# Delta-rule attention with a quick-GELU feed-forward on one core: scores, substitution and key normalization moved to other places of a slot

## The chip, the core and the metric

The kernel runs on one core of one Trainium2 chip. The metric is device time in microseconds (us) of one execution, the median of several runs. The core has a matrix engine (PE, with its weight loads shown apart as PEld), three engines for elementwise work (DVE, ACT, POOL) and DMA queues, which SP and ACT issue here. Each engine works off its own instructions in the order in which the program holds them, and waits on semaphores for the others.

## The reference

Two blocks, one behind the other. The first is delta-rule attention over 4 batches, 8 heads, 768 tokens and a head size of 48, with the keys normalized first:

```python
k_n = k / (np.linalg.norm(k, axis=-1, keepdims=True) + 1e-06)
state = np.zeros((B, H, D, D))
for t in range(S):
    kt, vt, bt = (k_n[:, :, t], v[:, :, t], beta[:, :, t, None])
    y[:, :, t] = np.einsum('bhd,bhde->bhe', q[:, :, t], state)
    v_old = np.einsum('bhde,bhd->bhe', state, kt)
    state = state + bt[:, :, :, None] * np.einsum('bhd,bhe->bhde', kt, vt - v_old)
```

The second takes the result as 3072 rows of 384 numbers:

```python
h = x @ w_in                                  # 384 x 2048
g = h * (1.0 / (1.0 + np.exp(-1.702 * h)))
return g @ w_out                              # 2048 x 384
```

q, k, v and beta are float32. w_in and w_out are float64, and the kernel turns them into float32 on its own engines.

## The kernel before

**Units and chunks.** The 768 tokens are cut into 6 chunks of 128, and a unit is one chunk of one batch with all 8 heads: 24 units, chunk by chunk, batch by batch. Inside a chunk the recursion becomes a triangular system, solved in 4 blocks of 32 rows.

**What a unit needs, in order.** Its keys (`KN`, 7 buffers) and queries (`QP`, 3 buffers) are loaded. `normalize` scales the keys: POOL squares them (`ksq`), DVE sums the squares (`ssq`), POOL takes the root with a power (`rn`), DVE adds 1e-6 and inverts, POOL multiplies. `prepare` is the scores of a unit. It transposes keys and queries on PE (`psT`), ACT copies them (`kqT`), PE forms key-key and key-query products in two halves (`psG`), ACT and DVE copy them (`G`), and two DMAs carry the key-key blocks through DRAM (`Nd`) into the layout `NT`. It is a generator that stops four times, after each transpose and after each half of the products. `invert` is the substitution, the inverse of the diagonal blocks. It is all DVE: one product with beta, 15 steps of product and sum, 8 larger products and sums, and a last product `YS` that goes out and back by DMA as `XB`. It is a generator of 25 stops, and one call serves two units.

**The sequence proper** is the class `Step`: `above` (products of earlier blocks, `psR`), `rest` (DVE subtracts, `V<-V,psR`), `solve` (PE, `psU`), `solved` (ACT copies to `U`), `queries`, `state` (`psS`, and DVE adds into `S_bd`) and `outputs` (`psY`, copied to `last` and `xT`).

**Slots.** `slot(n, share)` has six groups (places). It works on three units at once: the last two blocks and the state of unit n-1 (A), the second block of unit n (B_) and the first block of unit n+1 (D_). Beside them it puts the scores of unit n+4, steps of the substitution, the conversion of weights (early slots) and, from a queue, matmuls of the feed-forward (`hidden`, `ph`; `written`, `po`), 20.8 units of cost a slot in the long run. Before the change the scores stand in the first, second, fourth and fifth place; a substitution starts in the first place of each even slot with 4 stops a place, and what is left runs at the slot's end. Also at the end the next keys are loaded and normalized in one go.

**Order.** A scheduler merges this program order into one order for each engine. Calls wrapped in `pinned` keep their place in program order. So what an engine does in which order is read from the built kernel, not from the code alone.

**Start.** Four units are prepared first, then one substitution over all four (128 partitions) runs on DVE, while PE has only filler (`warm`). Keys of units 4 to 6 are loaded after that work's DMAs on SP; units 4 and 5 are normalized in a pinned block on DVE, unit 6 with `normalize`.

Of the kernel before, what the change touches and what calls it, by code (L numbers as in the profile page):

```python
# [18 lines left out]
def kernel(  # L19
# [19 lines left out]
    nc = tc.nc  # L39

    B, H, S, D = q.shape
# [10 lines left out]
    HB = 2  # L52
    GR = 6
# [22 lines left out]
    units = [(c, b) for c in range(NC) for b in range(B)]  # L76


    KN = [cpool.tile([128, H, DP], F32, name=f"KN{i}") for i in range(7)]
    QP = [cpool.tile([128, H, DP], F32, name=f"QP{i}") for i in range(3)]  # L80
# [5 lines left out]
    def load(n, pairs, dma=nc.sync.dma_start):  # L86
        c, b = units[n]
        for dst, src in pairs:
            dma(
                out=dst[n % len(dst)][:, :, 0:D],  # L90
                in_=src[b, :, c * C : (c + 1) * C, :].rearrange("h p d -> p h d"),
            )
# [9 lines left out]
    def pinned(op):  # L102

        return lambda *a, **kw: tc.keep_in_program_order(op(*a, **kw))  # L104
# [146 lines left out]
    ready = {}  # L251
    inverse = {}

    def normalize(n, mul):
        K = KN[n % len(KN)][:, :, 0:D]
        ksq = wk.tile([128, H, D], F32, tag="ksq", name="ksq", bufs=1)
        mul(ksq, K, K, op=ALU.mult)
        ssq = wk.tile([128, H], F32, tag="ssq", name="ssq", bufs=4)
        nc.vector.tensor_reduce(ssq, ksq, axis=AX.X, op=ALU.add)  # L259
        rn = wk.tile([128, H], F32, tag="rn", name="rn", bufs=4)  # L260
        nc.gpsimd.tensor_tensor(rn, ssq, half, op=ALU.pow)  # L261
        nc.vector.tensor_scalar(rn, rn, 1e-6, None, op0=ALU.add)
        nc.vector.reciprocal(rn, rn)
        mul(K, K, rn.broadcast_to([128, H, D]), op=ALU.mult)

    def normalize_first(b0):

# [7 lines left out]
        for b in range(HB):  # L275
            K = KN[(b0 + b) % len(KN)][:, :, 0:D]
            tt(sq[:, b], K, K, op=mult)
            red(s[:, b], sq[:, b], axis=AX.X, op=add)
# [9 lines left out]
        for b in range(HB):  # L288
            K = KN[(b0 + b) % len(KN)][:, :, 0:D]
            tt(K, K, s[:, b].broadcast_to([128, H, D]), op=mult)  # L290

# [138 lines left out]
    def bank(name, shape=(128, H, D)):  # L430
        return ps_seq.tile(list(shape), F32, tag="seq", name=name)
# [158 lines left out]
    def run(work):  # L590
        for _ in work:
            pass

    def ahead_of(work, n):
        for _ in range(n):
            next(work, None)

    steps, xTs, inverting, gT0 = {}, {}, iter(()), []

    def slot(n, share):  # L600

        nonlocal inverting
        A, B_, D_ = steps.pop(n - 1, None), steps.get(n), None
        P = prepare(n + B) if B <= n + B < len(units) else iter(())
        m = n - HB
        if m >= 0 and m % HB == 0 and m + B < len(units):  # L610
            inverting = invert(*units[m + B], HB)
        left = WB[n + 1] if n + 1 < len(WB) else 0
        todo = share
        for group in range(GR):
            if group == 0:
                if A:
                    for h in range(H):
                        A.above(2, h)
                    A.rest(2)
                next(P, None)  # L620
            elif group == 1:
                psU = bank("psU") if A else None
                for h in range(H):
                    if A:
                        A.solve(2, h, psU)
                    if B_:
                        B_.above(1, h)
                if A:
                    A.solved(2, psU)
                if B_:  # L630
                    B_.rest(1)
                next(P, None)
            elif group == 2:
                if A:
                    for h in range(H):
                        A.above(3, h)
                    A.rest(3)
                if n + 1 < len(units):
                    h = (n + 1) // HB
                    if h not in xTs:  # L640
                        xTs[h] = wk.tile([128, KC, NTH], F32, tag="xT", name="xT", bufs=3)
                    D_ = steps[n + 1] = Step(n + 1, xTs[h])
                    D_.keys()
                    D_.rest(0)
            elif group == 3:
                psU = bank("psU")
                turns = [(X, blk) for X, blk in ((A, 3), (B_, 1), (D_, 0)) if X]
                for h in range(H):
                    for X, blk in turns:
                        X.solve(blk, h, psU)  # L650
                for X, blk in turns:
                    X.solved(blk, psU)
                if A:
                    A.queries()
                next(P, None)
            elif group == 4:
                if A:
                    A.state()
                next(P, None)
                run(P)  # L660
            elif A:
                A.outputs()
            ahead_of(inverting, 4)
            more = left // (GR - group)
            run(weights(more))
            left -= more
            if queue:
                for cost in take(todo / (GR - group)):
                    todo -= cost
            if not queue and n <= HB:  # L670
                warm(NB0)
        if n + 1 == len(WB) - 1:
            run(weights(n_parts))
        run(inverting)
        if n > 0:
            if n - 1 + B < len(units):
                load_values(n - 1 + B)
            m = n - 1 + len(KN)
            if m < len(units):
                load(m, ((KN, k), (QP, q)), sync if n < B else nc.sync.dma_start)  # L680
                normalize(m, nc.gpsimd.tensor_tensor)
            h = (n - 1) // HB
            if h == 0:
                i = (n - 1) % HB
                queue.append(hidden(xTs[h], gT0, slice(i * C, (i + 1) * C), 0.67))
            if n % HB == 0:
                gT = gT0 if h == 0 else []
                if h > 0:
                    queue.append(hidden(xTs[h], gT, slice(0, NTH), 1.3))
                queue.append(written(*units[h * HB], gT))  # L690
                xTs.pop(h)

    queue = []
    sync = pinned(nc.sync.dma_start)
# [17 lines left out]
    nc.gpsimd.memset(S_bd, 0.0)  # L712
    for i in range(B, len(KN)):
        nc.gpsimd.memset(KN[i][:, :, D:DP], 0.0)
    for i in range(B, B + HB):
        load(i, ((KN, k), (QP, q)), sync)
    run(invert(0))
    normalize_first(B)
    for i in range(B + HB, len(KN)):
        load(i, ((KN, k), (QP, q)), sync)  # L720
        normalize(i, nc.gpsimd.tensor_tensor)
    run(weights(W1))
    for n in range(-1, len(units) + 1):

# [32 lines left out]
```

## Time and profile before

| what | value |
| --- | --- |
| median of 3 runs | 907.6 us (902.69 to 909.66) |
| the profiled execution | 905.0 us, its span 903.0 us |
| mean granted PE clock | 0.941 |
| PE busy | 829.3 us, 92% of the span |
| DVE busy | 499.7 us, 55% |
| ACT, POOL busy | 201.9 us, 105.0 us |
| DMA | 55.79 MB, mean 62 GB/s |

The profile records one execution. Busy time is the time in which an engine has an instruction under way. An idle stretch is put down to the engine or DMA that ended it, its releaser. The granted clock is the share of full speed that PE was given; in this profile it is 1 or 0.5, with changes between. Matmul ends are modelled, so PE's busy time is an upper bound of its work.

### The profile page before, as it was taken

How to read it: one execution, taken by the hardware profiler on the slowest of the kernel's cores; microseconds unless marked ns; L12 is line 12 of the kernel's file. 1: busy time of each engine (PE TensorE's matmuls, PEld its weight loads, DVE VectorE, ACT ScalarE, POOL GpSimd, SP SyncE). 2: the span in 40 equal slices, each digit the busy share in tenths (PEclk: the TensorE clock that was granted, in tenths of full speed). 3: DMA queues.
4: the chain of work that ended last, by engine and by line, in shares of the span. 5: the costliest groups of instructions: out<-in, count | busy, mean ns of one | idle time of the engine just before them, and what ended most of it. 6: DMA issues, size and time to landing. Idle time of an engine off the chain costs nothing.

```text
span 903.0 us, 15752 instructions
## 1 busy us (share of the span) xinstructions
PE 829.3 (92%) x6564; PEld 614.9 (68%) x6564; DVE 499.7 (55%) x1044; ACT 201.9 (22%) x387; POOL 105.0 (12%) x92
## 2 busy tenths in 40 slices
PE   8308999989999998998998998998999999999998
PEld 6206778657767766866866866866867767768684
DVE  7698749988993294285286286285286293110000
ACT  3102424332221311321311321321321312112020
POOL 2101101203112102102102102102100000000000
PEclk9658859999999998998999999998999999999999
DMA  9968235354213213213213213213202101000000
GB/s 176 212 83 136 85 91 130 96 124 101 37 40 82 50 36 73 49 36 74 49 28 82 49 28 81 50 33 67 49 20 65 41 19 34 4 20 3 12 9 19
DMA packets 164487, 55.79 MB, mean 62 GB/s; under 512 B 130112, under 2 KB 160064, under 8 KB 164416
## 3 DMA queue, kind: packets, MB, share of 16 engines
q1 hardware_dynamic: 158288, 53.57, 27.5%
q10 hardware_dynamic: 6128, 1.21, 1.1%
q8 instruction: 52, 0.85, 0.4%
q14 instruction: 19, 0.16, 0.1%
HBM read 33.13 MB, written 20.45 MB: 59 GB/s over the span
## 4 chain that ended last, share of the span: by engine, by line
PE 65%; DVE 24%; DMA 3%; issue 3%; POOL 3%; ACT 1%; SPq 1%; ACTq 0%; DVEq 0%
PE ph L536 24%; PE po L551 18%; PE psR L457 5%; DVE P L365 4%; PE psG L318 4%; PE psY L482 4%; PE psU L469 4%; PE psR L446 3%; POOL rn L261 2%; DVE NT L366 2%; DVE YB L366 2%; DVE YB L386 2%; PE psT L304 2%; DVE P L382 2%; PE psS L501 1%
## 5 line engine op out<-in xcount | busy, mean ns | idle before, releaser
L536 PE MATMUL ph<-xT,w_in 128*128 128x256 f32 (+1 forms) x1248 | 271.9, 375 | 0.0
L551 PE MATMUL po<-w_out,gT 128*128 128x384 f32 x768 | 268.3, 495 | 3.8 <-DVE w_out L176 3.8
L536 PEld LDWEIGHTS ph<-xT,w_in 128*128 128x128 f32 x1248 | 224.9, 196 | 35.1 <-issue 7.5
L551 PEld LDWEIGHTS po<-w_out,gT 128*128 128x128 f32 x768 | 140.9, 191 | 95.2 <-issue 9.4
L465 DVE TENSOR_TENSOR V<-V,psR 32x384 f32<-32x384 f32 x92 | 50.6, 550 | 132.7 <-PE psR L457 90.6
L541 ACT ACTIVATE gT<-ph 128x512 f32<-128x512 f32 (+1 forms) x104 | 58.6, 564 | 212.9 <-PE ph L536 212.9
L476 ACT COPY U<-psU 32x384 f32<-32x384 f32 x96 | 45.0, 469 | 197.7 <-PE psU L469 127.7
L342 POOL TENSOR_SCALAR_AFFINE_SELECT G<-G 128x1024 f32<-128x1024 f32 x24 | 28.9, 1204 | 414.8 <-issue 167.7
L457 PEld LDWEIGHTS psR<-U,G 32*32 32x32 f32 (+2 forms) x1152 | 58.4, 115 | 20.3 <-issue 19.1
L138 PE MATMUL ps_warm<-ident 128*128 128x256 bf16 x260 | 36.5, 298 | 37.0 <-DVE ps_warm L104 33.1
L318 PE MATMUL psG<-kqT 48*128 48x256 f32 x384 | 66.4, 434 | 4.0 <-ACT kqT L305 2.2
L469 PEld LDWEIGHTS psU<-V,XB 32*32 32x32 f32 x1536 | 39.5, 108 | 44.6 <-DVE V L465 22.0
L457 PE MATMUL psR<-U,G 32*32 32x48 f32 (+2 forms) x1152 | 68.9, 215 | 0.0
L469 PE MATMUL psU<-V,XB 32*32 32x48 f32 x1536 | 47.0, 208 | 20.4 <-DVE V L465 18.4
L326 DVE COPY G<-psG 128x512 f32<-128x512 f32 x44 | 30.3, 689 | 62.8 <-PE psG L318 62.2
L138 PEld LDWEIGHTS <-ident 128*128 128x128 bf16 x260 | 26.8, 106 | 45.4 <-DVE ps_warm L104 34.3
L382 DVE TENSOR_TENSOR P<-NT,YB 64x2 f32<-64x2 f32 (+4 forms) x150 | 49.9, 333 | 4.8
L386 DVE TENSOR_REDUCE YB<-P 64x2 f32<-64x2 f32 (+4 forms) x150 | 48.0, 320 | 4.7 <-DVE P L382 0.2
L318 PEld LDWEIGHTS psG<-kqT 48*128 48x128 f32 x384 | 39.4, 201 | 16.3 <-issue 4.7
L558 DVE COPY o<-po 128x384 f32<-128x384 f32 x24 | 13.3, 553 | 62.7 <-PE po L551 62.5
L322 ACT ACTIVATE G<-psG 128x512 f32<-128x512 f32 x48 | 28.6, 596 | 67.0 <-PE psG L318 65.6
L261 POOL TENSOR_TENSOR rn<-ssq,half 128x8 f32<-128x8 f32 x18 | 35.5, 1970 | 49.1 <-DVE ssq L259 49.1
(78 smaller groups left out, 682.7 us busy)
## 6 DMA issues: line engine op xcount, KB each, us to landing
Nd<-G SPq DMA_DIRECT2D x24, 512.0 KB, 3.5
w_out<-in_moe_w_out_dram SPq DMA_DIRECT2D x14, 384.0 KB, 3.1
KN<-in_k_dram SPq DMA_DIRECT2D x24, 192.0 KB, 2.7
w_out<-in_moe_w_in_dram SPq DMA_DIRECT2D x24, 192.0 KB, 4.4
V<-in_v_dram SPq DMA_DIRECT2D x24, 192.0 KB, 3.1
out_dram<-o SPq DMA_DIRECT2D x24, 192.0 KB, 2.0
QP<-in_q_dram SPq DMA_DIRECT2D x21, 192.0 KB, 3.7
NT<-Nd SPq DMA_DIRECT2D x24, 128.0 KB, 2.5
```

The source lines that it names most:

```text
L138: nc.tensor.matmul(ps, lhsT=ones[:, 0:128], rhs=ones, start=True, stop=True)
L261: nc.gpsimd.tensor_tensor(rn, ssq, half, op=ALU.pow)
L318: nc.tensor.matmul(ps[hh][:, i], lhsT=kqT[pr, g + i, 0, :], rhs=kqT[pr, g + i, :, :], start=True, stop=True,)
L382: tt(P, diag(Nf, i * BS, [[0, i], [1, i]]), diag(Yf, 0, [[BS, i], [1, i]]), op=ALU.mult,)
L386: red(diag(Yf, i, [[BS, i]]), P, axis=AX.X, op=ALU.add, negate=True)
L457: nc.tensor.matmul(self.psR[r, h, :], lhsT=self.G[a, h, 0, r], rhs=self.U[a, h, :], start=(self.c == 0 and h == 0), stop=True, skip_group_ ...
L465: nc.vector.tensor_tensor(self.V[r], self.V[r], self.psR[r], op=ALU.subtract)
L469: nc.tensor.matmul(psU[r, h, :], lhsT=self.XB[r, h, :], rhs=self.V[r, h, :], start=True, stop=True,)
L476: nc.scalar.copy(self.U[r], psU[r])
L536: nc.tensor.matmul(ph[:, u], lhsT=w_in[:, j, f * 128 : (f + 1) * 128], rhs=xT[:, j, t], start=(j == 0), stop=(j == KC - 1),)
L541: nc.scalar.activation(gT[f0 // FQ][:, f0 % FQ : f0 % FQ + 2, t], ph, ACT.Gelu_apprx_sigmoid)
L551: nc.tensor.matmul(po, lhsT=gT[f // FQ][:, f % FQ, i * C : (i + 1) * C], rhs=w_out[:, f, :], start=(f == 0), stop=(f == FC - 1),)
```

## The change

Four things are done together.

1. In `slot`, the scores of unit n+4 are brought forward: both transposes in the first place, the first half of the products in the second, the second half with its DMAs in the third. Nothing of them is left in the fourth and fifth.
2. A substitution begins in the last place of an odd slot with 5 stops, for units n+3 and n+4, and goes on with 4 stops a place in the even slot; what is left runs at the end of even slots only.
3. `normalize` becomes a generator with three stops: squares; sum and power; addition, reciprocal and product. Slot n takes one step of it a place, for unit n+5, whose keys were loaded at the end of slot n-1. Its products are always POOL's.
4. At the start, keys and queries of units 4 to 6 are loaded by ACT's queue ahead of the first substitution, and unit 6 is normalized in slot 1.

```diff
-    def normalize(n, mul):
+    def normalize(n):
         K = KN[n % len(KN)][:, :, 0:D]
+        mul = nc.gpsimd.tensor_tensor
         mul(ksq, K, K, op=ALU.mult)
+        yield 0.0
         nc.vector.tensor_reduce(ssq, ksq, axis=AX.X, op=ALU.add)
         nc.gpsimd.tensor_tensor(rn, ssq, half, op=ALU.pow)
+        yield 0.0
         nc.vector.tensor_scalar(rn, rn, 1e-6, None, op0=ALU.add)
...
+        yield 0.0
...
-        m = n - HB
-        if m >= 0 and m % HB == 0 and m + B < len(units):
-            inverting = invert(*units[m + B], HB)
+        m = n - 2 + len(KN)
+        K = normalize(m) if B + HB <= m < len(units) else iter(())
...
+                next(P, None)
                 next(P, None)
             elif group == 1:
...
                     D_.rest(0)
+                run(P)
             elif group == 3:
...
                     A.queries()
-                next(P, None)
             elif group == 4:
                 if A:
                     A.state()
-                next(P, None)
-                run(P)
             elif A:
                 A.outputs()
-            ahead_of(inverting, 4)
+            next(K, None)
+            if group == GR - 1 and n % HB == 1:
+
+                m = n + 1 + HB
+                if B <= m < len(units):
+                    inverting = invert(*units[m], HB)
+            ahead_of(inverting, 5 if n % HB == 1 else 4)
...
-        run(inverting)
+        if n % HB == 0:
+            run(inverting)
...
-                normalize(m, nc.gpsimd.tensor_tensor)
...
-    for i in range(B, B + HB):
-        load(i, ((KN, k), (QP, q)), sync)
+    for i in range(B, len(KN)):
+        load(i, ((KN, k), (QP, q)), pinned(nc.scalar.dma_start))
     run(invert(0))
     normalize_first(B)
-    for i in range(B + HB, len(KN)):
-        load(i, ((KN, k), (QP, q)), sync)
-        normalize(i, nc.gpsimd.tensor_tensor)
```

Three places of DVE's order show what the scheduler makes of it. Line numbers behind the change are 1 to 5 higher: `V<-V,psR` is L465 before and L469 after, `NT<-NT,bI` L358 and L362. P, YB, NT and YS belong to the substitution; ssq and rn to the normalization.

The first place is where an even slot passes into an odd one, in the long run. Before:

```order
L366 TENSOR_REDUCE YB<-P 64x16x4
L517 COPY last<-psY 48x128
L518 COPY xT<-psY 48x3x128
L366 TENSOR_REDUCE YB<-P 64x16x4
L259 TENSOR_REDUCE ssq<-ksq 128x8
L416 TENSOR_TENSOR YS<-YB,bI 64x1024
L262 TENSOR_SCALAR rn<-rn 128x8
L465 TENSOR_TENSOR V<-V,psR 32x384
L263 RECIPROCAL rn<-rn 128x8
L558 COPY o<-po 128x384
```

and after:

```order
L369 TENSOR_TENSOR P<-NT 64x1024
L370 TENSOR_REDUCE YB<-P 64x16x4
L420 TENSOR_TENSOR YS<-YB,bI 64x1024
L562 COPY o<-po 128x384
L513 TENSOR_TENSOR S_bd<-psS,S_bd 64x4x48 x2
L521 COPY last<-psY 48x128
L522 COPY xT<-psY 48x3x128
L261 TENSOR_REDUCE ssq<-ksq 128x8
L265 TENSOR_SCALAR rn<-rn 128x8
L266 RECIPROCAL rn<-rn 128x8
L469 TENSOR_TENSOR V<-V,psR 32x384
```

The end of the substitution has moved from behind the copies of the even slot's outputs to ahead of its state update; the subtraction V still stands behind one normalization.

The second place is the middle of an odd slot, where the copies of the scores (`G<-psG`) and the start of the next substitution (`NT<-NT,bI`) stand. Before:

```order
L326 COPY G<-psG 128x2x256
L509 TENSOR_TENSOR S_bd<-psS,S_bd 64x4x48 x2
L326 COPY G<-psG 128x2x256
L259 TENSOR_REDUCE ssq<-ksq 128x8
L262 TENSOR_SCALAR rn<-rn 128x8
L263 RECIPROCAL rn<-rn 128x8
L517 COPY last<-psY 48x128
L518 COPY xT<-psY 48x3x128
L465 TENSOR_TENSOR V<-V,psR 32x384
L358 TENSOR_TENSOR NT<-NT,bI 64x1024
```

and after:

```order
L469 TENSOR_TENSOR V<-V,psR 32x384
L330 COPY G<-psG 128x2x256
L469 TENSOR_TENSOR V<-V,psR 32x384 x2
L330 COPY G<-psG 128x2x256
L362 TENSOR_TENSOR NT<-NT,bI 64x1024
L386 TENSOR_TENSOR P<-NT,YB 64x2
L390 TENSOR_REDUCE YB<-P 64x2
L386 TENSOR_TENSOR P<-NT,YB 64x8
L513 TENSOR_TENSOR S_bd<-psS,S_bd 64x4x48 x2
```

The start of the substitution now follows the last copy of the scores directly, and the state update, the output copies and the next V stand behind it.

The third place is the start: the end of the first weight conversions and the begin of the substitution over four units (128 partitions). Before:

```order
L104 TENSOR_SCALAR tmp<-tmp 128x512 x2
L104 SCALAR_TENSOR_TENSOR tmp<-w_out,tmp 128x512
L104 SCALAR_TENSOR_TENSOR w_in<-w_in,tmp 128x512
L104 TENSOR_TENSOR NT<-NT,bI 128x1024
L104 TENSOR_TENSOR P<-NT,YB 128x2
```

and after:

```order
L104 SCALAR_TENSOR_TENSOR w_in<-w_in,tmp 128x512
L261 TENSOR_REDUCE ssq<-ksq 128x8
L265 TENSOR_SCALAR rn<-rn 128x8
L266 RECIPROCAL rn<-rn 128x8
L104 TENSOR_TENSOR NT<-NT,bI 128x1024
L104 TENSOR_TENSOR P<-NT,YB 128x2
```

The normalization of unit 6 has come ahead of the first substitution; before, it stood behind that and behind the pinned block of units 4 and 5.

## The prediction

> **What bounds the kernel now.** I read the engine totals first (PE busy 92% of the span), then busy time by stage, then PE's waits, then the instructions around the longest of them. By stage; the columns are stretch, length, busy us of PE, PEld, DVE, ACT and POOL with instruction counts, granted PE clock, DMA share, GB/s:
>
> ```profile
> 86.00:285.00 199.00, 188.26 (x1638) 140.31 (x1638) 162.23 (x341) 59.86 (x117) 34.15 (x26) 0.90 0.38 90
> 285.00:341.00 56.00, 56.00 (x437) 41.56 (x437) 29.43 (x64) 13.55 (x26) 6.91 (x6) 1.00 0.21 46
> 341.00:690.00 349.00, 334.73 (x2705) 247.85 (x2704) 195.42 (x388) 76.58 (x147) 50.46 (x40) 0.97 0.23 51
> ```
>
> PE is the bound from 285 us on: without a pause at first, and with 349.00 - 334.73 = 14.3 us of idle time and some lost clock between 341 and 690. PE's waits in 285 to 690 have a single entry (waiting, releaser, us, times, longest):
>
> ```profile
> PE psU L469 <- DVE V L465: 14.3, 5, 3.1
> ```
>
> So all of it is one event, five times: a solve waits for a subtraction on DVE. The timeline of the first one (start, us, engine):
>
> ```profile
> 341.96 0.86 PE L457 MATMUL psR<-U,G 64*32 64x48 f32 x16
> 343.25 2.75 PE L551 MATMUL po<-w_out,gT 128*128 128x384 f32 x8
> 344.93 0.55 DVE L259 TENSOR_REDUCE ssq<-ksq 128x8 f32<-128x384 f32 x1
> 345.52 1.22 DVE L416 TENSOR_TENSOR YS<-YB,bI 64x1024 f32<-64x1024 f32 x1
> 345.57 2.67 POOL L261 TENSOR_TENSOR rn<-ssq,half 128x8 f32<-128x8 f32 x1 [4.54 <-DVE ssq L259]
> 348.27 0.17 DVE L262 TENSOR_SCALAR rn<-rn 128x8 f32<-128x8 f32 x1 [1.53 <-POOL rn L261]
> 348.47 0.55 DVE L465 TENSOR_TENSOR V<-V,psR 32x384 f32<-32x384 f32 x1
> 349.08 0.23 PE L469 MATMUL psU<-V,XB 32*32 32x48 f32 x1 [3.08 <-DVE V L465]
> ```
>
> psR was there at 342.8, but V ran at 348.5: in front of it DVE had ssq, the last product YS of the substitution and a wait for POOL's power. PE's cover, the eight po matmuls, ended at 346.0. The price is more than the idle time. From the end of that cover to the end of the 24 ph matmuls behind it, at the five stalls and at the one boundary (689.13) that has no substitution any more:
>
> ```profile
> 346.00:360.57 14.57, 11.49 (x84) 10.01 (x85) 3.33 (x7) 1.66 (x3) 3.07 (x2) 0.77 0.32 64
> 415.85:429.76 13.91, 11.41 (x84) 10.18 (x85) 2.75 (x7) 1.66 (x3) 2.49 (x2) 0.75 0.34 67
> 485.03:497.99 12.96, 9.88 (x84) 8.75 (x85) 3.33 (x7) 1.67 (x3) 3.07 (x2) 0.87 0.35 73
> 553.26:564.04 10.78, 8.27 (x85) 7.44 (x85) 2.76 (x7) 1.67 (x3) 2.50 (x2) 1.00 0.43 86
> 619.32:633.86 14.54, 11.46 (x84) 10.05 (x85) 3.33 (x7) 1.67 (x3) 3.06 (x2) 0.77 0.25 51
> 689.13:697.33 8.20, 8.20 (x84) 7.36 (x85) 1.66 (x3) 1.66 (x3) 0.00 (x0) 1.00 0.44 90
> ```
>
> The same work takes 8.20 us undisturbed; the five sum to 66.76, so the stalls cost 66.76 - 5 x 8.20 = 25.8 us: 14.3 idle, 11.5 from the clock that is halved after four of them.
>
> **The long run, part by part.** *Substitution begun earlier.* DVE's order now has YS ahead of the even slot's state update, so that the V of the odd slot stands behind output copies and one normalization only. For this the scores must be there in time:
>
> ```profile
> 337.62 0.69 DVE L326 COPY G<-psG 128x512 f32<-128x512 f32 x1
> 338.38 0.37 SPq L330 DMA_DIRECT2D Nd<-G  x1
> 341.60 0.34 SPq L336 DMA_DIRECT2D NT<-Nd  x1
> DMA to landing us min/median/max: 2.4/2.5/2.7
> 373.65 0.69 DVE L326 COPY G<-psG 128x512 f32<-128x512 f32 x1 [0.38 <-PE psG L318]
> 381.58 1.22 DVE L358 TENSOR_TENSOR NT<-NT,bI 64x1024 f32<-64x1024 f32 x1
> ```
>
> From the last G copy's end (338.3) to NT's landing are 341.6 + 2.5 - 338.3 = 5.8 us. In the odd slot at 373.65 DVE did not begin until 381.58, 7.2 us behind the copy. Now the copy comes two places earlier, some 10 us of a slot of 32, and NT follows it directly: DVE waits about 5.8 us at its head and then starts roughly 12 us earlier than before. Behind that wait stand S_bd, last and xT, which PE first feeds in the fifth and sixth place; the wait lies mostly beside the solves of the fourth place, where DVE has nothing else. I cost it at nothing; if NT lands later than some 6 us beyond that, it holds the outputs and the next V (rival E). The backlog of 3.1 us at the odd slot's V is gone with 12 us to spare, less the pieces of normalization now ahead of it.
>
> *Keys normalized step by step.* Same instructions, other places. In an even slot the sums of squares stand ahead of last, xT and V, and the keys are loaded only once the state matmuls of the odd slot have freed their buffer.
>
> ```profile
> KN<-in_k_dram SPq DMA_DIRECT2D x24, 192.0 KB, 2.7
> L261 POOL TENSOR_TENSOR rn<-ssq,half 128x8 f32<-128x8 f32 x18 | 35.5, 1970 | 49.1 <-DVE ssq L259 49.1
> 373.58 2.79 PE ph L536 x12
> 338.17 1.08 PE L482 MATMUL psY<-G,U 128*48 128x128 f32 x16
> 342.76 0.66 PE L304 MATMUL psT<-ident,KN 128*128 128x128 f32 x4
> ```
>
> From the end of psS: load 2.7, squares 0.83, ssq 0.55, power 1.97, rn, last and xT 1.0, five substitution pieces about 1.7, V 0.55, and about 1 us of semaphores and issue: 10.3 us. PE has in that stretch, by its new order, three blocks of twelve ph (8.4), four po (half of 2.75), the outputs (1.08), above (0.86) and both transposes (1.3): 13.0 us. The slack is 2 to 3 us, the smallest that I find, and it is what is late next. I leave 2 us of residual stalls over five pairs; the ends are 0 and five stalls like the cheapest above, 5 x (10.78 - 8.20) = 12.9.
>
> POOL's normalization now runs beside the substitution. The last large product of the substitution, beside which POOL squares and selects at the end of an even slot, and an earlier one of the same size without (count, busy us, mean ns):
>
> ```profile
> L365 DVE TENSOR_TENSOR P<-NT 64x1024 f32<-64x1024 f32 x10 | 15.3, 1530 | 0.0
> L365 DVE TENSOR_TENSOR P<-NT,YB 64x1024 f32<-64x1024 f32 x10 | 12.2, 1219 | 0.3
> ```
>
> That is 0.31 us more for a product, within the slack. The Trainium skill, "SBUF — State Buffer", section "SBUF: two separate sides", speaks against the change here: a GpSimd instruction and a VectorE instruction with two SBUF inputs hold a shared port in turn, each for its whole length. By that rule alone POOL's two normalizations of a pair could hold DVE for their whole length instead of for fractions of it, and the residual would rise from 2 us to rival B's 12.9; the rows show the growth, but only a part of such a length.
>
> *Scores forward.* PE, ACT and DVE do the same work in other places: nothing added, and the copies of G have the wait of the fourth place behind them.
>
> **The start.** Here is a cost. Rows of the start before:
>
> ```profile
> 33.23 0.60 ACT L322 ACTIVATE G<-psG 128x512 f32<-128x512 f32 x1 [1.11 <-PE psG L318]
> 42.20 1.22 DVE L104 TENSOR_TENSOR NT<-NT,bI 128x1024 f32<-128x1024 f32 x1
> 75.15 1.05 SPq L104 DMA_DIRECT2D KN<-in_k_dram  x1
> 81.88 0.82 POOL L257 TENSOR_TENSOR ksq<-KN 128x384 f32<-128x384 f32 x1 [46.63 <-DMA KN<-in_k_dram]
> 82.74 0.55 DVE L259 TENSOR_REDUCE ssq<-ksq 128x8 f32<-128x384 f32 x1 [2.10 <-POOL ksq L257]
> 83.37 2.03 POOL L261 TENSOR_TENSOR rn<-ssq,half 128x8 f32<-128x8 f32 x1 [0.66 <-DVE ssq L259]
> 85.64 0.55 DVE L465 TENSOR_TENSOR V<-V,psR 32x384 f32<-32x384 f32 x1
> 86.21 0.20 DVE L263 RECIPROCAL rn<-rn 128x8 f32<-128x8 f32 x1
> 86.24 0.94 PE L469 MATMUL psU<-V,XB 32*32 32x48 f32 x32 [2.55 <-DVE V L465]
> ```
>
> Unit 6's normalization held DVE and V there, and PE 2.55 us. It now stands ahead of the first substitution, on which everything waits. ssq to reciprocal took 86.41 - 82.74 less 0.55 for V = 3.1 us. Its load is the fifth on ACT's queue, free from 33.83. At 75.15, beside other loads, one took 81.88 - 75.15 = 6.7 us; issued at about 35.5, behind four others of some 0.4 each, it lands at 42.2, and the squares end at 43.1, 0.9 us behind DVE's 42.2. So I add 3.1 + 0.9 = 4.0 us (bounds 0, if NT is as late by itself, and 7, if the loads share the queues with the scores' DMAs) and take off the 2.6: +1.4.
>
> **Stage 86 to 285.** DVE is busy 162 of 199 us and its substitutions release PE; PE is idle 199.00 - 188.26 = 10.7 us, and the clock of 0.90 means 0.20 x 199 = 40 us at half. The order is quite another here. Substitutions begin earlier but meet the same weight conversions; units 1 and 2 lose scores that lay between their solves, and DVE waits for NT. Bounds: nothing gained, or all 10.7 and some 9 of the 20 us that half clock can cost. I take half of the idle time, -5, as the work on DVE is unchanged.
>
> **The sum.** -25.8 + 2 + 1.4 - 5 = -27.4. The profiled execution took 905.0 us (span 903.0 and 2.0 around it) and becomes 877.6; it lies 2.6 below the median of 907.6, so the forecast is 880 us.
>
> **Rivals.** A, the forecast: the five stalls go. 0.60.
>
> B, the wait moves: the even slot's V, behind the load, squares and power of that slot's keys, is late in every pair. For: the slack is small. Against: 10.3 us of work under 13.0 of cover. It decides once the keys land some 3 us later than 2.7. Residual 12.9 in place of 2: 891 us. 0.14.
>
> C, the clock stays low: only the idle time goes. For: the drop at 415.85 follows the same 2.5 us of idle time as at 553.26, where there is none. Against: the boundary at 689.13 has the same small matmuls at full clock. Gain 14.3 in place of 25.8: 891.5 us. 0.07. The Trainium skill, "TensorE: Matmul & The Clock Gate", Part 1, leans to C: it wants idleness of about a whole window of 3.4 us before the clock halves, and the windows run free. Stalls of 2.5 to 3.1 us would then not be the cause, yet four of five here are followed by half clock.
>
> D, the start loses 7 - 2.6 = 4.4 and the early stage gains nothing: +3 and +5 on the forecast, 888 us. 0.08.
>
> E, slower: the wait for NT at DVE's head. SP issues Nd and NT behind output DMAs, and every row behind L362 waits with it. Before, 5.2 us a pair were lost (25.8 / 5). To end above 916.7 the new wait must cost 9.1 + 25.8 = 35 us, 7 a pair, which needs NT to land 5.8 + 6 + 7 = 19 us behind the copy; all measured landings are within 2.7 us. 920 us. 0.04.
>
> F, no change: the stalls are merely re-dealt. About 905 us. 0.07.
>
> **Chances.** A change of under 1% (9 us) can hardly be told from none for this kernel. Faster holds A to D but for the tails of B to D: 0.87. Same: F and such tails, 0.08. Slower: 0.05. The range holds A and most of B to D, 0.8 together. Its low end is the forecast less the early stage's other half and the clock, 5 + 9: 866; the high end is B with D, 891 + 8 = 899.
>
> **What would show it.** Right: between 341 and 660 PE idle under 4 us, clock 1.00, no wait of psU for V; L362 some 6 us behind the second G copy; pairs of slots 63.5 us apart (now 69.85 from 346.00 to 415.85, less 6.4). The first substitution begins at 45 to 47 us instead of 42.2, and no wait for rn near 83. Wrong: psU waiting for V in even slots (B), clock 0.5 without idle time (C), long idle time of DVE before L362 with PE idle too (E), PE idle above 10 us between 86 and 285.

## The result and the profile after

| what | before | after |
| --- | --- | --- |
| median | 906.6 us (4 runs, 902.69 to 909.66) | 875.0 us (4 runs, 870.02 to 880.94) |
| ratio, 95% interval | | 0.966 (0.957 to 0.974) |
| profiled execution, its span | 905.0, 903.0 us | 870.0, 868.0 us |
| mean granted PE clock | 0.941 | 0.969 |
| PE, DVE busy | 829.3, 499.7 us | 803.2, 502.0 us |

A second measurement, further down, gave 872.3 us and a ratio of 0.960 (0.956 to 0.964). The forecast was 880 in a range of 866 to 899. The profiled execution of the changed kernel is the fastest of its four, with a mean clock of 0.969; the others lie between 0.953 and 0.965.

The table of stages of the changed kernel, same stretches and columns as in the prediction:

```profile
86.00:285.00 199.00, 183.39 (x1715) 138.03 (x1716) 164.61 (x342) 62.11 (x123) 36.43 (x26) 0.98 0.40 94
285.00:341.00 56.00, 56.00 (x477) 40.65 (x476) 36.90 (x73) 13.81 (x27) 7.90 (x7) 1.00 0.27 59
341.00:690.00 349.00, 349.00 (x2904) 258.79 (x2903) 206.28 (x420) 82.98 (x160) 42.37 (x38) 1.00 0.23 52
```

Between 285 and 690 PE has neither a pause nor a halved clock. In the early stage, 86 to 285, the two parts of the loss went opposite ways: idle time rose from 10.7 to 199.00 - 183.39 = 15.6 us, while the clock rose from 0.90 to 0.98. That is the surprise of this result.

Rows picked from the timeline of the changed kernel where the first stall was, as an even slot passes into an odd one (start, us, engine):

```profile
324.63 0.28 PE L505 MATMUL psS<-U,KN 128*128 128x96 f32 x1
324.94 1.22 DVE L420 TENSOR_TENSOR YS<-YB,bI 64x1024 f32<-64x1024 f32 x1
...
331.52 0.83 POOL L258 TENSOR_TENSOR ksq<-KN 128x384 f32<-128x384 f32 x1 [11.88 <-DMA KN<-in_k_dram]
332.38 0.55 DVE L261 TENSOR_REDUCE ssq<-ksq 128x8 f32<-128x384 f32 x1 [2.33 <-POOL ksq L258]
332.96 2.75 PE L555 MATMUL po<-w_out,gT 128*128 128x384 f32 x8
333.01 1.64 POOL L263 TENSOR_TENSOR rn<-ssq,half 128x8 f32<-128x8 f32 x1 [0.67 <-DVE ssq L261]
335.12 0.55 DVE L469 TENSOR_TENSOR V<-V,psR 32x384 f32<-32x384 f32 x1
335.54 1.46 PE L540 MATMUL ph<-xT,w_in 128*128 128x256 f32 x6
336.93 0.23 PE L473 MATMUL psU<-V,XB 32*32 32x48 f32 x1
```

YS now runs 10 us ahead of V. The wait for POOL's power is still there, and V still stands behind it; but V ends at 335.67 and PE has po and ph until its solve at 336.93. 1.3 us of slack are left here; one pair of slots later they are 2.5.

The waits at DVE's head for NT, from the timeline of DVE:

```profile
282.36 0.69 DVE L330 COPY G<-psG 128x512 f32<-128x512 f32 x1 [0.56 <-PE psG L322]
288.82 1.22 DVE L362 TENSOR_TENSOR NT<-NT,bI 64x1024 f32<-64x1024 f32 x1 [5.77 <-DMA NT<-Nd]
...
352.27 1.22 DVE L362 TENSOR_TENSOR NT<-NT,bI 64x1024 f32<-64x1024 f32 x1 [5.64 <-DMA NT<-Nd]
...
416.01 1.22 DVE L362 TENSOR_TENSOR NT<-NT,bI 64x1024 f32<-64x1024 f32 x1 [5.79 <-DMA NT<-Nd]
```

DVE waits 5.6 to 5.8 us behind the copy, PE does not. Pairs of slots are 63.45 and 63.74 us apart.

And the start of the changed kernel:

```profile
43.33 0.82 POOL L258 TENSOR_TENSOR ksq<-KN 128x384 f32<-128x384 f32 x1 [7.89 <-DMA KN<-in_k_dram]
46.70 0.20 DVE L266 RECIPROCAL rn<-rn 128x8 f32<-128x8 f32 x1
46.88 1.22 DVE L104 TENSOR_TENSOR NT<-NT,bI 128x1024 f32<-128x1024 f32 x1
72.55 1.22 DVE L420 TENSOR_TENSOR YS<-YB,bI 128x1024 f32<-128x1024 f32 x1
87.76 0.55 DVE L469 TENSOR_TENSOR V<-V,psR 32x384 f32<-32x384 f32 x1
```

Unit 6's normalization holds the first substitution until 46.88 (42.20 before); of these 4.7 us, 87.76 - 85.64 = 2.1 are left at the first V.

### The profile page after: what moved, and what is told of

It is laid out like the page before. It is cut to its first block, busy times and chain, and to the rows that moved or that the text cites. A ratio compares the mean times of both kernels' runs of the same rounds, so it can differ in the third digit from the quotient of the medians.

```text
span 868.0 us, 15729 instructions
## 1 busy us (share of the span) xinstructions
PE 803.2 (93%) x6564; PEld 593.0 (68%) x6564; DVE 502.0 (58%) x1044; ACT 200.0 (23%) x387; POOL 100.2 (12%) x92
## 4 chain that ended last, share of the span: by engine, by line
PE 81%; DVE 12%; DMA 3%; issue 1%; SPq 1%; POOL 1%; ACTq 1%; ACT 0%; DVEq 0%; POOLq 0%
PE po L555 28%; PE ph L540 27%; PE psY L486 5%; PE psG L322 5%; PE psR L461 4%; PE psU L473 4%; PE psR L450 2%; PE psT L308 2%; PE psS L505 2%; DVE P L104 1%; DMA w_out<-in_moe_w_in_dram 1%; DVE YB L104 1%; DMA bI<-in_beta_dram 1%; DVE tmp L175 1%; SPq L236 1%
## 5 line engine op out<-in xcount | busy, mean ns | idle before, releaser
L540 PE MATMUL ph<-xT,w_in 128*128 128x256 f32 (+1 forms) x1248 | 267.5, 369 | 2.3 <-ACT gT L545 2.3
L540 PEld LDWEIGHTS ph<-xT,w_in 128*128 128x128 f32 x1248 | 218.9, 191 | 39.5 <-issue 10.1
L469 DVE TENSOR_TENSOR V<-V,psR 32x384 f32<-32x384 f32 x92 | 50.6, 550 | 93.8 <-PE psR L461 87.4
L346 POOL TENSOR_SCALAR_AFFINE_SELECT G<-G 128x1024 f32<-128x1024 f32 x24 | 31.3, 1303 | 311.0 <-DVE G L330 202.4
L461 PEld LDWEIGHTS psR<-U,G 32*32 32x32 f32 (+2 forms) x1152 | 52.7, 107 | 20.9 <-issue 20.1
L322 PE MATMUL psG<-kqT 48*128 48x256 f32 x384 | 60.9, 416 | 2.0 <-ACT kqT L309 1.4
L461 PE MATMUL psR<-U,G 32*32 32x48 f32 (+2 forms) x1152 | 62.7, 205 | 0.0
L473 PEld LDWEIGHTS psU<-V,XB 32*32 32x32 f32 x1536 | 37.2, 105 | 23.8 <-issue 12.1
L473 PE MATMUL psU<-V,XB 32*32 32x48 f32 x1536 | 44.7, 203 | 0.8 <-DVE V L469 0.8
L322 PEld LDWEIGHTS psG<-kqT 48*128 48x128 f32 x384 | 37.3, 194 | 11.5 <-ACT kqT L309 2.7
L521 DVE COPY last<-psY 48x128 f32<-48x128 f32 x24 | 7.1, 295 | 60.4 <-ACT xT L522 59.4
```

What stands on the lines that cost most here:

```text
L322: nc.tensor.matmul(ps[hh][:, i], lhsT=kqT[pr, g + i, 0, :], rhs=kqT[pr, g + i, :, :], start=True, stop=True,)
L461: nc.tensor.matmul(self.psR[r, h, :], lhsT=self.G[a, h, 0, r], rhs=self.U[a, h, :], start=(self.c == 0 and h == 0), stop=True, skip_group_ ...
L469: nc.vector.tensor_tensor(self.V[r], self.V[r], self.psR[r], op=ALU.subtract)
L473: nc.tensor.matmul(psU[r, h, :], lhsT=self.XB[r, h, :], rhs=self.V[r, h, :], start=True, stop=True,)
L540: nc.tensor.matmul(ph[:, u], lhsT=w_in[:, j, f * 128 : (f + 1) * 128], rhs=xT[:, j, t], start=(j == 0), stop=(j == KC - 1),)
```

## Experiments: which part does it

Each run was timed together with the kernel before, and every ratio is to it, with its 95% interval. Line numbers in its rows are its own, a few off those above.

**Part 3 alone.** The generator `normalize` with three stops, one step a place; unit 6 stays at the start:

```diff
...
+        m = n - 2 + len(KN)
+        K = normalize(m) if len(KN) <= m < len(units) else iter(())
...
+            next(K, None)
...
-                normalize(m, nc.gpsimd.tensor_tensor)
...
```

> The kernel before with part 3 alone: normalization in three steps, one a place (unit 6 normalized at the start as before). The substitution begins where it did, the scores stay where they were. In the built order V of the odd slot now stands directly behind YS and ahead of the additions on rn; before, it stood behind the wait for POOL's power. Theory 1, the stall is the wait for the power that stands ahead of V: from the rows of before, YS ends at 346.74 and V can run at once, the solve at 347.4 instead of 349.1 with the same end of cover at 346.0, so some 1.4 us of idle time stay of 3.1, too short to be followed by half clock as often. Five stalls of about 1.4: 7 us instead of 25.8, so about 19 us less than the kernel before, 886 to 890 us. Theory 2, the stall is the substitution that ends too late, and takes what the normalization leaves: all five stalls stay above 2.5 us and the time within 5 us of the kernel before. Early stage: no change expected by either.

Measured: 882.0 us, ratio 0.970 (0.967 to 0.974). The timeline of DVE, and the waits of PE from 285 us on, of this run:

```profile
340.93 1.22 DVE L420 TENSOR_TENSOR YS<-YB,bI 64x1024 f32<-64x1024 f32 x1
342.07 0.55 DVE L469 TENSOR_TENSOR V<-V,psR 32x384 f32<-32x384 f32 x1
343.68 0.17 DVE L265 TENSOR_SCALAR rn<-rn 128x8 f32<-128x8 f32 x1 [1.06 <-POOL rn L263]
```

```profile
PE psU L473 <- DVE V L469: 5.4, 5, 1.3
```

The substitution ends as late as ever, directly ahead of V. Only the wait for POOL's power moved from ahead of V to behind it, and 14.3 us of idle time became 5.4. Theory 1 holds for the long run: from the KN transposes (`psT<-ident,KN`) ahead of the first stall to those five pairs later PE took 685.89 - 342.76 = 343.1 us before and 662.90 - 338.16 = 324.7 here, 18.4 less, against about 19. The time is 4 us under its range: the first stall's place was reached 342.76 - 338.16 = 4.6 us earlier, and neither theory expected anything of the early stage. Its clock is 0.93 instead of 0.90; why is not shown.

**Part 2 alone.** The substitution is begun in the last place of an odd slot:

```diff
-            inverting = invert(*units[m + B], HB)
...
+            if group == GR - 1 and n % HB == 1:
+                m = n + 1 + HB
+                if B <= m < len(units):
+                    inverting = invert(*units[m], HB)
+            ahead_of(inverting, 5 if n % HB == 1 else 4)
```

> The kernel before with part 2 alone: the substitution is begun in the last place of the odd slot with 5 stops, scores and normalization as before. In the built order its first product still follows the V of the next slot, since NT comes late; what changes is that YS stands one place earlier and that V stands ahead of the additions on rn. Theory 1 (the wait for the power ahead of V): like part 3 alone, 886 to 890 us. Theory 2 (the substitution must really start earlier, for which the scores are needed): as the kernel before, 900 to 910 us.

Measured: 912.7 us, ratio 1.005 (1.002 to 1.009): nearer to theory 2, whose range ended at 910, but not by its way. PE's waits from 285 us on, of this run, and then two rows of its busy time by stretch:

```profile
PE psU L469 <- DVE V L465: 6.9, 5, 1.6
```

```profile
354.00:370.00 16.00, 16.00 (x121) 11.98 (x116) 3.27 (x7) 3.07 (x6) 1.20 (x2) 0.51 0.29 56
494.00:508.00 14.00, 14.00 (x110) 10.33 (x109) 3.27 (x7) 2.91 (x6) 0.84 (x2) 0.51 0.32 65
```

The idle time was halved, more or less as theory 1 said, but the kernel did not get faster: behind two of the three stalls of 1.6 us, PE ran 16 and 14 us without a pause at half clock. The five pairs took 692.23 - 348.45 = 343.8 us, as long as before. Idle time saved was given back as clock.

**Parts 1 and 2, without 3 and 4.**

```diff
+                next(P, None)
                 next(P, None)
             elif group == 1:
...
                     D_.rest(0)
+                run(P)
...
                     A.queries()
-                next(P, None)
...
                     A.state()
-                next(P, None)
-                run(P)
```

and the diff of part 2.

> Parts 1 and 2 together, the normalization and the start as in the kernel before. In the built order of the long run every instruction on DVE stands as in the changed kernel. Theory 1 of my prediction, the substitution that ends 10 us earlier frees V, and part 3 does nothing of its own: no wait of psU for V from 285 us on, 25 us less there, and the start without the 4 us that unit 6 costs; 870 to 878 us. Rival, the stepwise normalization is what makes it fit: the waits for the power come back, one or more us at each pair, 885 to 895 us.

Measured: 876.9 us, ratio 0.964 (0.959 to 0.969).

**Part 1 alone**, only the diff just shown.

> Part 1 alone in the kernel before: scores in the first, second and third place, substitution code, normalization and start as before. In the built order of the long run every engine already has the order of the changed kernel: the substitution, written for the first place of an even slot, is moved up behind the scores by the scheduler. Theory 1, the scores forward carry the gain and parts 2 and 3 are consequences that the scheduler draws by itself: no wait of psU for V from 285 us on, no half clock from 115 to 138 us, 872 to 880 us. Rival, parts 2 or 3 do something of their own here: five waits come back in part, 885 to 900 us.

Measured: 871.4 us, ratio 0.958 (0.952 to 0.964). The last stretch of the table of stages, in this run:

```profile
341.00:690.00 349.00, 349.00 (x2912) 259.87 (x2912) 205.79 (x417) 83.51 (x161) 41.95 (x38) 1.00 0.24 53
```

The scores forward do it all. In the timeline of DVE of this run the substitution's end stands ahead of the even slot's state update and copies, as in the changed kernel:

```profile
329.63 1.22 DVE L416 TENSOR_TENSOR YS<-YB,bI 64x1024 f32<-64x1024 f32 x1
...
331.47 0.72 DVE L509 TENSOR_TENSOR S_bd<-psS,S_bd 64x192 f32<-64x192 f32 x2
```

So once NT is early, the scheduler moves the substitution up although the code still begins it in the even slot; with part 2 and late scores it brought YS only ahead of xT and ssq (350.38 against 351.51 and 352.10). That it goes by what is ready fits both orders, and is not shown further. Parts 2 and 3 add nothing measurable to part 1.

## Experiments: what the clock costs

**Filler in the stalls.** The kernel before, with 24 matmuls that compute nothing used, ahead of solves that wait. DVE's order is untouched, V is as late as ever:

```diff
+            if group == 0 and n % HB == 1 and 13 <= n <= 21:
+                warm(24)
             ahead_of(inverting, 4)
```

> The kernel before with 24 filler matmuls on PE (2.6 us at full clock, they compute nothing that is used) in each of the five odd slots whose first solve waits for V. On DVE and ACT the order is that of the kernel before, so V is as late as ever; on PE three ph matmuls (about 0.7 us) come in front of the solve too. Theory, the clock is halved because PE idles: the idle time becomes filler, the half clock behind it goes, worth the 11.5 us of my prediction, and the three ph give about 0.7 us at each of five places, 3 us: 14 us less than the kernel before, 893 to 897 us, clock 1.00 between 341 and 690. Rival C of the prediction, half clock has another cause (the many small matmuls at that place): clock and time stay, 903 to 911 us.

Measured: 904.2 us, ratio 0.993 (0.990 to 0.996). The slots were counted wrong: the first two stalls got no filler, and two places that needed none got some. So the time tells little; but one execution now holds both kinds, the two unfilled stalls in the first row and the three filled in the second:

```profile
341.00:476.00 135.00, 129.40 (x1032) 96.72 (x1031) 70.71 (x142) 29.79 (x57) 20.75 (x16) 0.94 0.23 50
476.00:690.00 214.00, 214.00 (x1759) 158.05 (x1758) 127.32 (x249) 47.37 (x91) 32.27 (x25) 1.00 0.24 54
```

**Filler in all five**, `9 <= n <= 17` in the same diff:

> The kernel before with 24 filler matmuls on PE in the odd slots of all five stalls (in the run before this one they stood two pairs too late: three stalls were filled, two places got filler without need, two stalls stayed). From that run a filler takes 2.63 us and six ph matmuls, 1.4 us, come in front of the solve with it, which together cover the 2.5 to 3.1 us. Theory, idle time is what halves the clock: 25.8 us of cost are replaced by 5 x 2.63 = 13.1 us of filler, 12.7 us less than the kernel before, 895 to 900 us, clock 1.00 between 285 and 690. Rival C, half clock comes whatever PE does there: 14.3 us of idle time are replaced by 13.1 us of filler, 1 us less, 905 to 912 us, and the rows behind the five places show clocks of 0.75 to 0.87.

Measured: 891.7 us, ratio 0.982 (0.977 to 0.987), so 17.5 us less by the medians, with an interval of about 11 to 21 by the ratio. The long run of the profiled execution:

```profile
341.00:690.00 349.00, 349.00 (x2946) 260.34 (x2946) 197.24 (x391) 79.67 (x152) 50.65 (x40) 1.00 0.24 53
```

PE spends 13 us on nothing, where it had idled 14.3, and the kernel is 11 to 21 us faster. The five pairs, taken as with part 3 alone, last 673.47 - 342.87 = 330.6 us instead of 343.1: 12.5 less, against 12.7 by the theory. Only the clock can pay for that. Filler closes the gap and is dense work too, so this run alone can't tell the two apart; but the changed kernel has no filler and no gap there, and its clock stays at 1.00 over the same small matmuls. Rival C is gone: without the gaps there was no half clock in the long run. A gap is not enough for it, though, as the stall of 2.5 us behind 553.26 shows.

**Filler in slot 2.** The early stage before has 24 us at half clock, from 114.6 to 138.5. It begins behind two gaps of PE of 0.80 and 0.76 us:

```profile
112.99 0.70 PE L318 MATMUL psG<-kqT 48*128 48x256 f32 x2 [0.80 <-ACT kqT L305]
114.45 0.23 PE L469 MATMUL psU<-V,XB 32*32 32x48 f32 x1 [0.76 <-DVE V L465]
```

The kernel before with

```diff
+            if group == 0 and n == HB:
+                warm(16)
             ahead_of(inverting, 4)
```

> The kernel before with 16 filler matmuls (1.8 us at full clock) in the first place of slot 2, in front of the solve that waited 0.76 us for V at 114.45, behind which the clock was half for 24 us. Theory, the early gain of the change is the clock of this stretch and two short gaps start it: with the filler the clock stays 1.00 there, the small matmuls of slot 2 take half their time, some 8 to 10 us less for 1 us more of filler; part of it may be lost again to the weight conversions on DVE, 898 to 905 us against 908 us. Rival, the clock falls because the small matmuls are not dense enough, whatever stands in front: half clock from about 116 to 138 us again, 908 to 911 us.

Measured: 902.8 us, ratio 0.995 (0.991 to 0.999). The same stretch in the kernel before, and then in this run:

```profile
114.00:138.00 24.00, 22.76 (x225) 18.36 (x226) 12.55 (x32) 6.33 (x12) 2.09 (x2) 0.51 0.33 81
```

```profile
114.00:138.00 24.00, 21.91 (x281) 19.57 (x280) 19.09 (x52) 10.14 (x22) 5.57 (x4) 1.00 0.45 102
```

The same small matmuls run at full clock, and DVE gets 19.09 us of its work into the stretch instead of 12.55, as PE feeds it faster. The gain at the end, 1 to 8 us by the interval, is smaller than half of 24 us. Why is not shown. In the profiled execution PE ran at half clock from about 170 to 177, where before it did not, and was idle 13.4 us between 86 and 285 instead of 10.7; DVE's weight conversions, which stand in this stage, may hold it too.

How much the clock weighs in all can be read from the kernel before alone. Over its 43 executions that were run beside these kernels the mean clock lies between 0.927 and 0.950 and the span between 912.7 and 897.4 us; a straight line through them gives 5.9 us of span for 0.01 of clock (correlation -0.85). 0.01 is 18 us at half clock in 905, so such a microsecond goes with about a third of itself over the whole kernel. In the prediction's rows of the five stalls it cost half of itself: some 24 us at half clock, 11.5 us lost. There PE was the only bound.

## Experiments: the start

**The start as before**, all else as changed:

```diff
-        K = normalize(m) if B + HB <= m < len(units) else iter(())
+        K = normalize(m) if len(KN) <= m < len(units) else iter(())
...
-    for i in range(B, len(KN)):
-        load(i, ((KN, k), (QP, q)), pinned(nc.scalar.dma_start))
+    for i in range(B, B + HB):
+        load(i, ((KN, k), (QP, q)), sync)
     run(invert(0))
     normalize_first(B)
+    for i in range(B + HB, len(KN)):
+        load(i, ((KN, k), (QP, q)), sync)
+        run(normalize(i))
```

> The changed kernel with the start as before: keys of units 4 to 6 loaded after the first four units' DMAs on SP, unit 6 normalized behind the first substitution. Theory, unit 6's normalization ahead of the first substitution costs what the traces show at the first V, 2.1 us: the first substitution begins at 42 instead of 46.9, YS 4.7 us earlier, the first V in slot 0 waits some 2 us for rn again; 870 to 874 us against 875 us. Rival, the later work is bound by the loads and the conversions that stand beside it and takes the gain back, or the early stage falls into half clock again: 875 to 885 us.

Measured: 869.4 us, ratio 0.957 (0.954 to 0.960), not apart from the changed kernel's. The first substitution begins at 42.99 and YS at 68.22, 4.3 us earlier than in the changed kernel. But of that only 0.2 us arrive at the first V:

```profile
84.57 2.03 POOL L263 TENSOR_TENSOR rn<-ssq,half 128x8 f32<-128x8 f32 x1 [0.67 <-DVE ssq L261]
86.64 0.17 DVE L265 TENSOR_SCALAR rn<-rn 128x8 f32<-128x8 f32 x1 [1.54 <-POOL rn L263]
87.55 0.55 DVE L469 TENSOR_TENSOR V<-V,psR 32x384 f32<-32x384 f32 x1
90.22 2.07 PE L322 MATMUL psG<-kqT 48*128 48x256 f32 x6 [4.51 <-DVE G L330]
```

Unit 6's normalization now stands ahead of V and of the copy of G behind it. Each start pays for unit 6, only at another place.

**Unit 6 late.** The loads behind the first units' DMAs, and the normalization of unit 6 left to slot 1:

```diff
-    for i in range(B, len(KN)):
-        load(i, ((KN, k), (QP, q)), pinned(nc.scalar.dma_start))
+    for i in range(B, B + HB):
+        load(i, ((KN, k), (QP, q)), sync)
     run(invert(0))
     normalize_first(B)
+    for i in range(B + HB, len(KN)):
+        load(i, ((KN, k), (QP, q)), sync)
```

> The changed kernel with one thing undone: the keys of units 4 to 6 are loaded behind the first four units' DMAs on SP, as before; the normalization of unit 6 stays in slot 1. In the built order it now stands behind the first V and two copies of G; in the changed kernel it stands ahead of the first substitution, and with the start as before ahead of the first V. Theory, what is left to gain at the start is both losses, 4.7 us ahead of the substitution and the 4.5 us that the scores waited for a copy of G behind that V: 865 to 869 us. Rival, the first solves wait for the weight conversions or the clock falls in another place: 869 to 876 us.

Measured: 863.8 us, ratio 0.950 (0.947 to 0.953), the fastest of all. The first V and unit 6's sum, by the timeline of this run:

```profile
85.01 0.55 DVE L469 TENSOR_TENSOR V<-V,psR 32x384 f32<-32x384 f32 x1
...
92.47 0.57 DVE L261 TENSOR_REDUCE ssq<-ksq 128x8 f32<-128x384 f32 x1
```

The sum stands 7 us behind V, where nothing waits for it. The first V is 2.75 us earlier than in the changed kernel and the span 7.2 us shorter (860.8); the rest came in the early stage, where the clock is 0.99 and PE is idle 12.8 us.

The changed kernel was run again beside two others:

> The changed kernel again, beside the two others of this call on one chip. By its first result 870 to 881 us, ratio to the kernel before 0.957 to 0.974; by both theories of the start it lies 8 to 12 us above the version with unit 6's normalization late (863.8 us). Below 868 us that difference would not hold.

Measured: 872.3 us, ratio 0.960 (0.956 to 0.964), apart from the 0.947 to 0.953 of the version with unit 6 late.

**Part 1 and unit 6 late.** The kernel before with part 1, `normalize(i, ...)` taken from the start, and in `slot`

```diff
+        if n == 0:
+            normalize(B + HB, nc.gpsimd.tensor_tensor)
         if n > 0:
```

> Part 1 alone in the kernel before, and unit 6 normalized at the end of slot 0 instead of at the start. In the built order the first V now stands ahead of unit 6's sum, the long run is as with part 1 alone. Theory, parts 2 and 3 are worth nothing beside part 1, and the 4.4 us that the scores waited behind the first V go: 863 to 868 us. Rival, part 3 with its steps is needed in the early slots, where the weight conversions stand on DVE: 868 to 876 us.

Measured: 867.1 us (863.12 to 875.3), ratio 0.954 (0.950 to 0.959). Its interval overlaps with those of both other versions, so whether the steps of part 3 help in the early slots stays open. In its profiled execution, the slowest of six, there is again a stretch at half clock in which PE hardly pauses. It follows a gap of 1.64 us, in which PE waited for POOL's last product on the keys:

```profile
192.00:218.00 26.00, 25.88 (x114) 16.03 (x115) 15.55 (x42) 4.65 (x10) 4.76 (x5) 0.50 0.14 34
```

## Why the prediction was right, and where it was not

**The five stalls: right in place and size.** From the end of the cover at the first stall to the end at the place five pairs later, the kernel before took 689.13 - 346.00 = 343.1 us. In the changed kernel the same eight po end at 335.71 and, five pairs later, at 653.82: 318.1. That is 25.0 us, against 25.8 less 2. Of the residual of 2 us nothing shows: PE does not wait.

**The clock's share of it: right.** 11.5 of the 25.8 were put down to half clock. With filler in place of the gaps the sum by the prediction's own terms is 25.8 - 13.1 = 12.7; the five pairs gave 12.5.

**Which part does it: incomplete.** The prediction read the new order rightly, but gave the substitution's earlier start as its cause, with scores as a condition, and the steps of the normalization as a cost. The runs show that the scores alone are enough and part 2 alone is worth nothing. It also named the wait for the power only in passing. Part 3 alone leaves the substitution where it was and takes 14.3 us of idle time down to 5.4, so most of each stall goes if V stands ahead of that wait. But the substitution was behind the wait as well: at the first stall the squares were ready at 345.57 - 4.54 = 341.0, and DVE came to their sum only at 344.93, behind pieces of the substitution. The two stood in a row, and moving either frees most of it.

**The wait for NT: right.** 5.8 us and 63.5 us a pair were forecast, 5.6 to 5.8 and 63.45 to 63.74 came, and PE did not wait. Rival E is out.

**The slack: right at the even slot, far too large at the odd one.** For the V of the even slot, the one of rival B, 10.3 us of work under 13.0 of cover were forecast, 2 to 3 to spare. Rows picked from the timeline after:

```profile
355.69 1.03 PE L505 MATMUL psS<-U,KN 128*128 128x96 f32 x8
365.96 0.55 DVE L469 TENSOR_TENSOR V<-V,psR 32x384 f32<-32x384 f32 x1
368.76 0.23 PE L473 MATMUL psU<-V,XB 32*32 32x48 f32 x1
```

From psS's end at 356.72 V takes 366.51 - 356.72 = 9.8 us, the cover is 368.76 - 356.72 = 12.0, and 2.25 are left. The V of the odd slot was said to have 12 us to spare less the normalization ahead of it, and has 1.3: in the rows further up psS ends at 324.91 and V at 335.67, 10.8 us under 336.93 - 324.91 = 12.0. What takes the rest is the normalization, for which the prediction gave no number there, and SP's queue makes it late:

```profile
326.78 0.36 SPq L563 DMA_DIRECT2D out_dram<-o  x1
327.19 0.89 SPq L424 DMA_DIRECT2D Yd<-YS  x2
328.18 0.39 SPq L89 DMA_DIRECT2D KN<-in_k_dram  x1
```

The load of the keys stands behind the output and the substitution's result, which the substitution now delivers earlier, and is issued 3.3 us after psS. No piece of a substitution lies in front of this V, and that made up for it.

**POOL beside the substitution.** Said: 0.31 us more for a product. The largest product did not suffer (1217 ns); a smaller one did. Groups of DVE after, and the same product before:

```profile
L369 DVE TENSOR_TENSOR P<-NT 64x512 f32<-64x512 f32 x10 | 11.5, 1146 | 0.0
```

```profile
L365 DVE TENSOR_TENSOR P<-NT 64x512 f32<-64x512 f32 x10 | 6.8, 681 | 0.0
```

One such product, and POOL's select of G beside it:

```profile
318.55 1.09 POOL L346 TENSOR_SCALAR_AFFINE_SELECT G<-G 128x1024 f32<-128x1024 f32 x1 [15.69 <-DVE G L330]
318.78 1.40 DVE L369 TENSOR_TENSOR P<-NT 64x512 f32<-64x512 f32 x1
```

The select ends at 319.64. A product of 0.68 us that had to wait for the select would end at 320.32, and it ended at 320.18. Here the wait is nearly the whole of what was left of the select, as the Trainium skill, "SBUF — State Buffer", section "SBUF: two separate sides", has it, and not the part of it that the prediction read from its rows. On the mean it is 0.47 us more for this product; two larger ones are shorter than before by 0.31 us (1530 to 1217 ns) and 0.30 (1250 to 948), so the large products lost nothing in sum.

**The start: right, a little small.** +4.0 was said for the first substitution and +4.7 came; +1.4 was said in all, and the first V is 2.1 us later.

**Stage 86 to 285: the step that failed.** "I take half of the idle time, -5". Up to the end of the first cover the changed kernel is 346.00 - 335.71 = 10.3 us ahead, 12.4 if the 2.1 at the first V are taken off; and idle time grew by 4.9. The gain is the clock's, so the term had the right sign for a reason that did not hold: half clock fell from 0.10 x 2 x 199 = 40 us to 0.02 x 2 x 199 = 8. The prediction had the clock only in its lower bound, at "some 9 of the 20 us". By the third of a microsecond that the 43 executions give, I estimate 32 us less at half clock as about 11 us. Slot 2 shows where: its small matmuls ran from 114.6 to 134.1 at half clock before, and in the changed kernel at full clock. The first ph starts at 118.1 and not at 134.1; 4.5 of these 16 us were there ahead of the slot's first solve (109.97 against 114.45), and some small matmuls now stand behind the ph. The filler in slot 2 showed that the clock there goes with the gaps ahead of it, and the place of the scores decides on these gaps. In all five profiled executions with late scores and no filler there (before, part 2, part 3, both runs with filler in the stalls), PE has the gaps of 0.80 and 0.76 to 0.77 us, and a clock of 0.54 to 0.61 between 114 and 140. In all seven with early scores, the changed kernel twice among them, that clock is 0.87 to 1.00. In the rest of the stage nothing of the kind is shown: parts 1 and 2 together have stretches at half clock in other places, and the same kernel has more or less of it from one execution to the next.

The sum gave 877.6 us for the profiled execution, and it took 870.0: 7.4 more from the early stage, 1.2 more from the long run, 0.7 less at the start and 0.3 less behind the last cover are the 7.6. Some of this is luck of the execution, the fastest of its four at the highest clock. The medians differ by 5 us from the forecast (7.7 in the second measurement).

## What to carry to other kernels

In these traces a gap of one to three microseconds on PE had to be priced with the clock behind it, not by its length: look at the granted clock of the stretch that follows, and if a gap can't be removed, filler matmuls in it can pay. Where a scheduler sets the order, ask which data is late rather than where the code begins a piece of work: early scores moved the substitution, and an early start in the code did not. A step on a path is not paid off by moving it ahead: unit 6's normalization cost 2 to 5 us by the traces at either of two places, and nothing where the engine had time.

## What the runs showed of the hardware

Half clock can outlast the gap ahead of it by far while PE hardly pauses: 16 and 14 us in the run with part 2 alone, behind gaps of 1.60 and 1.61 us, and 26 us in that with part 1 and unit 6 late, behind 1.64. Most of the matmuls in these stretches are small ones for scores and solves (psR, psU, psY, psG); the 26 us also hold po in groups of four, and the 16 and the 14 us end with ph at half clock. Not each gap is followed by it: of the three of 1.6 us with part 2 alone, two are. The Trainium skill, "TensorE: Matmul & The Clock Gate", Part 1, has the clock halved after about a window of 3.4 us of idleness and restored after one of activity; here gaps of 1.6 us, and in slot 2 two of 0.8 us, were followed by half clock, and 16 us of PE that is busy by the profile did not restore it. What activity does is not shown by these runs.
